# A long scan as a tree of block matmuls, a convolution as a 64-wide-tile transform, and a computed instruction order

## The chip, the cores and the metric

The kernel runs on one core of one Trainium2 chip. The metric is the device time of one execution in microseconds (us). The kernel before takes 355.92 us (median of 2 runs, 354.24 to 357.6). Profiled executions are quoted by their span, from the first to the last instruction, which is some 2 us shorter than the time. TensorE's clock is not constant: the profile gives the granted share of full speed, and each run is marked fast or slow from it and from the other runs of the same kernel.

## The reference

Two independent sequence mixers read inputs of 2048 steps x 640 channels, and their results stand side by side in the output.

```python
# part A: diagonal complex state space model, 640 states, 2048 steps
Lam_bar = exp(dt * (Lambda_re + 1j * Lambda_im))
B_bar   = ((Lam_bar - 1) / Lam)[:, None] * Bmat
Bu      = einsum("bld,pd->blp", x, B_bar)
h       = Lam_bar * h + Bu[:, t, :]            # for every t, in order
y_A     = 2 * einsum("blp,dp->bld", hseq, Cmat).real + x * Dskip

# part B: four shift taps, a gate, a causal convolution over all 2048 steps
k_shift = sum_t k[t - j] * shift_k[:, j]       # j = 0..3
kv      = k_shift * v
y_B     = q * (causal_conv(kv, ssm_k) + kv * ssm_D)
```

## The kernel before

Part A runs as 5 state tiles x 4 chunks of 512 steps. In each block TensorE multiplies by B, ScalarE copies the result out of PSUM (where the matmuls put their sums), and VectorE turns the complex decay into a real one (rotate by cosines and sines, scan 512 steps, rotate back). Then TensorE projects with C.

```python
def block(self, j, c):                         # 20 of these (cut)
    for k in range(NT):
        nc.tensor.matmul(pz[:, 0, :], lhsT=self.BTre[:, k, j * 128:(j + 1) * 128], rhs=xT[:, k, :], ...)
    ...                                        # the same for BTim
    nc.scalar.copy(out=z[:], in_=pz[:])
    nc.vector.tensor_tensor(out=t1[:], in0=cosT, in1=zre, op=ALU.mult)
    ...                                        # six such 512-wide operations
    nc.vector.tensor_tensor_scan(out=ure[:], data0=rb, data1=wre[:], initial=ini_re, ...)
    nc.vector.tensor_tensor_scan(out=uim[:], data0=rb, data1=wim[:], initial=ini_im, ...)
    ...                                        # six more to rotate back: hre, him
```

Part B is a 4096-point transform of the padded sequence in two stages, and VectorE does the taps and the products.

```python
for j in (2, 1, 0):                            # taps
    nc.vector.scalar_tensor_tensor(out=kvT[:], in0=kT[:, PAD - j:PAD - j + L], scalar=sk[:, j:j + 1], in1=kvT[:], ...)
...
nc.tensor.matmul(pa[:, i, :], lhsT=st[:, d8, a_lo * 128:(a_lo + 1) * 128], rhs=self.C.R[:, a_lo, :], ...)  # 128x512
nc.scalar.copy(out=As[...], in_=pa[...])
```

The order of instructions is that of the program, which mixes blocks of part A into part B after a fixed pattern.

Of the kernel before, what the change touches and what calls it, by code (L numbers as in the profile page):

```python
# [9 lines left out]
ALU = mybir.AluOpType  # L10
ACT = mybir.ActivationFunctionType
# [3 lines left out]
PI = float(np.pi)  # L15
TWO_PI = float(2 * np.pi)
MAGIC = 12582912.0
SC = float(2 * np.pi / 2 ** 32 * (1 - 2 ** -22))
NFFT = 4096

L = 2048
D = 640
NT = 5
CW = 512
NCH = L // CW
PAD = 16
PGROUPS = [[0, 16, 1, 2], [3, 4, 5, 6], [7, 8, 9, 10], [11, 12, 13, 14], [15]]
PLANE_POS = {k1: i for i, k1 in enumerate([0, 16] + list(range(1, 16)))}


class BConstants:

    def __init__(self, nc, cpool, tpool, hpi_col):
        self.nc, self.cpool, self.tp, self.hpi = nc, cpool, tpool, hpi_col
        g, v = nc.gpsimd, nc.vector
        self.pidx_i = tpool.tile([128, 1], i32, name="pidx_i")
        g.iota(self.pidx_i[:], pattern=[[0, 1]], base=0, channel_multiplier=1)
        self.plo_i = tpool.tile([128, 1], i32, name="plo_i")
        v.tensor_single_scalar(out=self.plo_i[:], in_=self.pidx_i[:], scalar=7, op=ALU.bitwise_and)
        self.phi_i = tpool.tile([128, 1], i32, name="phi_i")  # L40
        v.tensor_single_scalar(out=self.phi_i[:], in_=self.pidx_i[:], scalar=3, op=ALU.arith_shift_right)
        self.c20 = tpool.tile([128, 1], i32, name="c20")
        g.iota(self.c20[:], pattern=[[0, 1]], base=2 ** 20, channel_multiplier=0)
        self.c27 = tpool.tile([128, 1], i32, name="c27")
        g.iota(self.c27[:], pattern=[[0, 1]], base=2 ** 27, channel_multiplier=0)

    def _cos(self, out_ap, ph, shape, tag):
        aph = self.tp.tile(shape, f32, name=f"{tag}_aph")
        self.nc.scalar.activation(out=aph[:], in_=ph, func=ACT.Abs, scale=SC)
        self.nc.scalar.activation(out=out_ap, in_=aph[:], func=ACT.Sin, bias=self.hpi[:, 0:1], scale=-1.0)  # L50

    def _kq_iota(self, shape, pat_slot, pat_part, tag):
        g, tp = self.nc.gpsimd, self.tp
        kcol = tp.tile(shape, i32, name=f"{tag}_kcol")
        g.iota(kcol[:], pattern=pat_slot, base=0, channel_multiplier=0)
        q8 = tp.tile(shape, i32, name=f"{tag}_q8")
        g.iota(q8[:], pattern=pat_part, base=0, channel_multiplier=0)
        return kcol, q8

    def build_R(self):  # L60
        nc, tp, g = self.nc, self.tp, self.nc.gpsimd
        sh = [128, 16, 2]
        kcol, q8 = self._kq_iota(sh, [[1, 16], [0, 2]], [[0, 16], [8, 2]], "r")
        g.iota(kcol[:, 0:1, 1:2], pattern=[[0, 1], [0, 1]], base=16, channel_multiplier=0)
        g.iota(q8[:, 0:1, 1:2], pattern=[[0, 1], [0, 1]], base=0, channel_multiplier=0)
        gcol = tp.tile([128, 16], i32, name="r_gcol")
        g.iota(gcol[:], pattern=[[1, 16]], base=0, channel_multiplier=0)
        mask = tp.tile([128, 16], bf16, name="r_mask")
        nc.vector.tensor_tensor(out=mask[:], in0=gcol[:], in1=self.phi_i[:, 0:1].to_broadcast([128, 16]), op=ALU.is_equal)

        def bc(t):
            return t[:, 0:1].to_broadcast([128, 32]).rearrange("p (s t) -> p s t", s=16)

        a2 = tp.tile([128, 1], i32, name="r_a2")
        g.tensor_tensor(out=a2[:], in0=self.plo_i[:], in1=self.plo_i[:], op=ALU.add)
        m = tp.tile(sh, i32, name="r_m")
        g.tensor_tensor(out=m[:], in0=kcol[:], in1=bc(a2), op=ALU.mult)
        g.tensor_tensor(out=m[:], in0=m[:], in1=q8[:], op=ALU.add)
        self.R = self.cpool.tile([128, 2, 512], bf16, name="R")
        for a_lo in range(2):  # L80
            if a_lo == 1:
                g.tensor_tensor(out=m[:], in0=m[:], in1=kcol[:], op=ALU.add)
            ph = tp.tile(sh, i32, name="r_ph")
            g.tensor_tensor(out=ph[:], in0=m[:], in1=bc(self.c27), op=ALU.mult)
            cv = tp.tile([128, 32], bf16, name="r_cv")
            self._cos(cv[:].rearrange("p (s t) -> p s t", s=16), ph[:], sh, "r")
            g.tensor_tensor(out=self.R[:, a_lo, :].rearrange("p (g k) -> p g k", k=32),
                            in0=cv[:].rearrange("p (o k) -> p o k", o=1).to_broadcast([128, 16, 32]),
                            in1=mask[:].rearrange("p (g o) -> p g o", o=1).to_broadcast([128, 16, 32]), op=ALU.mult)

    def build_G(self):
        nc, tp, g = self.nc, self.tp, self.nc.gpsimd
        bsh = tp.tile([128, 1], i32, name="g_bsh")
        nc.vector.tensor_single_scalar(out=bsh[:], in_=self.pidx_i[:], scalar=20, op=ALU.logical_shift_left)
        self.Gre = self.cpool.tile([128, 17, 128], bf16, name="Gre")
        self.Gim = self.cpool.tile([128, 17, 128], bf16, name="Gim")
        self.nGim = self.cpool.tile([128, 15, 128], bf16, name="nGim")
        for (p0, p1) in ((0, 3), (3, 6), (6, 9), (9, 12), (12, 15), (15, 17)):
            n = p1 - p0
            sh = [128, n, 128]  # L100
            v = tp.tile([128, 3, 128], i32, name="t_v")
            g.iota(v[:, 0:n, :], pattern=[[1, n], [32, 128]], base=p0, channel_multiplier=0)
            ph = tp.tile([128, 3, 128], i32, name="t_ph")
            g.tensor_tensor(out=ph[:, 0:n, :], in0=v[:, 0:n, :], in1=bsh[:, 0:1].to_broadcast([128, n * 128]).rearrange(
                "p (a b) -> p a b", a=n), op=ALU.mult)
            nc.scalar.activation(out=self.Gim[:, p0:p1, :], in_=ph[:, 0:n, :], func=ACT.Sin, scale=-SC)
            q0 = max(p0, 1)
            q1 = min(p1, 16)
            nc.scalar.activation(out=self.nGim[:, q0 - 1:q1 - 1, :], in_=ph[:, q0 - p0:q1 - p0, :], func=ACT.Sin, scale=SC)
            aph = tp.tile([128, 3, 128], f32, name="t_aph")  # L110
            nc.scalar.activation(out=aph[:, 0:n, :], in_=ph[:, 0:n, :], func=ACT.Abs, scale=SC)
            nc.scalar.activation(out=self.Gre[:, p0:p1, :], in_=aph[:, 0:n, :], func=ACT.Sin, bias=self.hpi[:, 0:1], scale=-1.0)

    def build_H(self):
        nc = self.nc
        self.Hre = self.cpool.tile([128, 17, 128], bf16, name="Hre")
        self.nHim = self.cpool.tile([128, 17, 128], bf16, name="nHim")
        self.Him = self.cpool.tile([128, 15, 128], bf16, name="Him")
        nc.sync.dma_start_transpose(out=self.Hre[:], in_=self.Gre[:])
        nc.sync.dma_start_transpose(out=self.nHim[:], in_=self.Gim[:])  # L120
        nc.sync.dma_start_transpose(out=self.Him[:], in_=self.nGim[:])

    def build_Mq(self):
        nc, tp, g, v = self.nc, self.tp, self.nc.gpsimd, self.nc.vector
        kap = tp.tile([128, 4], i32, name="m_kap")
        g.iota(kap[:], pattern=[[8, 4]], base=0, channel_multiplier=0)
        g.tensor_tensor(out=kap[:], in0=kap[:], in1=self.plo_i[:, 0:1].to_broadcast([128, 4]), op=ALU.add)
        slot = tp.tile([128, 4], i32, name="m_slot")
        v.tensor_single_scalar(out=slot[:], in_=kap[:], scalar=1, op=ALU.arith_shift_right)
        part = tp.tile([128, 4], i32, name="m_part")  # L130
        v.tensor_single_scalar(out=part[:], in_=kap[:], scalar=1, op=ALU.bitwise_and)
        eq1 = tp.tile([128, 4], i32, name="m_eq1")
        v.tensor_single_scalar(out=eq1[:], in_=kap[:], scalar=1, op=ALU.is_equal)
        kcol = tp.tile([128, 4], i32, name="m_kcol")
        v.tensor_single_scalar(out=kcol[:], in_=eq1[:], scalar=4, op=ALU.logical_shift_left)
        v.tensor_tensor(out=kcol[:], in0=kcol[:], in1=slot[:], op=ALU.add)
        q8 = tp.tile([128, 4], i32, name="m_q8")
        v.tensor_tensor(out=q8[:], in0=part[:], in1=eq1[:], op=ALU.subtract)
# [13 lines left out]
        def bq(t):  # L152
            return t[:].rearrange("p (q o) -> p q o", o=1).to_broadcast(sh3)
# [15 lines left out]
class PartA:  # L169
# [155 lines left out]
    def block(self, c, j, base0=None):  # L325
# [67 lines left out]
        if j == NT - 1:  # L393
            self.project(c)
# [308 lines left out]
```

## Time and profile before

| kernel before, profiled span 354.2 us | TensorE | VectorE | ScalarE | GpSimd |
|---|---|---|---|---|
| busy, us | 235.3 | 282.7 | 173.1 | 85.3 |

The next lines are from the page of the kernel before: busy time of each engine with its share of the span, then three rows of the strip in which each digit is the busy share, in tenths, of one fortieth of the span (8.9 us), or the granted TensorE clock in tenths, then the shares of the chain of waits.

```profile
span 354.2 us, 5098 instructions
...
PE 235.3 (66%) x1896; PEld 150.7 (43%) x1896; DVE 282.7 (80%) x619; ACT 173.1 (49%) x231; POOL 85.3 (24%) x99
...
PE   0058179303799874757898198588499997675591
DVE  3809999984999999998970799999974896989502
PEclk9998859856699999699999789589699999699698
...
issue 36%; DVE 24%; POOL 12%; PE 9%; SPq 8%; DMA 6%; ACT 3%; ACTq 1%; POOLq 0%; DVEq 0%
```

VectorE (DVE) is the limit: row after row of nines, and the engine with the largest busy share. TensorE (PE) is busy for 66% of the span; its longest wait in total is for VectorE, as the next lines show.

Two groups of the same page show what TensorE waits for, and one more thing that is easy to overlook. A group line gives busy time, mean ns of one instruction, and the idle time before it with the engine that ended it.

```profile
L406 PE MATMUL psA<-Csre,hre 128*128 128x320 bf16 x160 | 49.2, 330 | 40.8 <-DVE hre L388 21.0
...
L161 POOL TENSOR_TENSOR m_cv<-m_cv,m_coef 128x64 f32<-128x64 f32 x1 | 25.2, 25237 | 4.1 <-ACT m_cv L50 4.1
```

The projection waits 21.0 us for the rotated state on VectorE. And one GpSimd (POOL) multiply of 128x64 elements took 25.2 us beside a full VectorE.

### The profile page before, as it was taken

To read this page: it belongs to the slowest core of one execution; us is meant where nothing else is said; L and a number is where in the kernel's file an instruction comes from. 1 tells how busy PE (TensorE), PEld (TensorE's weight loads), DVE (VectorE), ACT (ScalarE), POOL (GpSimd) and SP (SyncE) were. 2 spreads that over 40 slices of the span, in tenths; PEclk is the share of its full clock that TensorE was granted. 3 is DMA by queue.
4 is the path that set the end of the run, shared out by engine and by line. 5 is a ranking of instruction groups with operands and counts; after the bars stand their busy time and mean duration, and the time that the engine had idled before them with its cause. 6 is when DMAs were issued, how large, how long until landed. Compare 5 with 4: busy or idle time off the path is not lost.

```text
span 354.2 us, 5098 instructions
## 1 busy us (share of the span) xinstructions
PE 235.3 (66%) x1896; PEld 150.7 (43%) x1896; DVE 282.7 (80%) x619; ACT 173.1 (49%) x231; POOL 85.3 (24%) x99
## 2 busy tenths in 40 slices
PE   0058179303799874757898198588499997675591
PEld 0013055301564542544655065265286554464371
DVE  3809999984999999998970799999974896989502
ACT  3548748303357484246564216478254795245020
POOL 2943639993120000020210001001041000020021
PEclk9998859856699999699999789589699999699698
DMA  5999997101035544283757704020664012232312
GB/s 95 197 209 213 205 213 150 44 0 61 19 102 141 112 105 108 71 161 64 179 137 153 170 1 121 20 71 30 148 166 149 1 31 54 66 102 61 76 57 78
DMA packets 89802, 36.68 MB, mean 104 GB/s; under 512 B 76465, under 2 KB 86706, under 8 KB 89778
## 3 DMA queue, kind: packets, MB, share of 16 engines
q1 hardware_dynamic: 65330, 18.01, 25.6%
q0 software_dynamic: 3808, 13.11, 12.5%
q10 hardware_dynamic: 20640, 5.24, 6.5%
q8 instruction: 15, 0.25, 0.3%
q14 instruction: 9, 0.07, 0.1%
HBM read 9.19 MB, written 6.55 MB: 44 GB/s over the span
## 4 chain that ended last, share of the span: by engine, by line
issue 36%; DVE 24%; POOL 12%; PE 9%; SPq 8%; DMA 6%; ACT 3%; ACTq 1%; POOLq 0%; DVEq 0%
POOL m_cv L161 7%; DVE kvT L495 4%; DVE uim L377 2%; PE psB L452 2%; DVE ure L376 2%; SPq L483 2%; DMA Zt<-Zs 2%; DMA out_dram<-yo 2%; PE psB L593 2%; SPq L500 1%; PE psA L406 1%; DMA vT<-in_B_v_dram 1%; PE psA L407 1%; SPq L209 1%; ACTq L583 1%
## 5 line engine op out<-in xcount | busy, mean ns | idle before, releaser
L406 PE MATMUL psA<-Csre,hre 128*128 128x320 bf16 x160 | 49.2, 330 | 40.8 <-DVE hre L388 21.0
L352 PE MATMUL psA<-xT,BTre 128*128 128x512 bf16 x100 | 31.1, 417 | 32.5 <-DMA xT<-in_A_x_dram 20.9
L407 PE MATMUL psA<-Csimn,him 128*128 128x320 bf16 x160 | 49.1, 327 | 1.3 <-DVE him L391 1.2
L337 POOL DMA_DIRECT2D tbase<-trig_tab x15 | 10.8, 721 | 120.4 <-DVE sct L348 75.5
L535 ACT CAST Xs<-psB 128x1024 bf16<-128x1024 f32 (+1 forms) x25 | 21.9, 886 | 36.1 <-PE psB L475 18.5
L358 ACT CAST z<-psA 128x1024 bf16<-128x1024 f32 x20 | 20.1, 1014 | 26.4 <-PE psA L355 15.5
L407 PEld LDWEIGHTS <-him 128*128 128x128 bf16 x160 | 16.7, 105 | 30.2 <-issue 18.7
L406 PEld LDWEIGHTS <-hre 128*128 128x128 bf16 x160 | 16.4, 105 | 30.2 <-DVE hre L388 24.4
L352 PEld LDWEIGHTS <-BTre 128*128 128x128 bf16 x100 | 10.1, 104 | 43.6 <-issue 25.6
L593 PE MATMUL psB<-Mq,Zt 128*128 128x256 bf16 x160 | 24.3, 323 | 6.6 <-DMA Zt<-Zs 6.6
L452 PE MATMUL psB<-R,h_st 128*128 128x512 bf16 x80 | 24.6, 449 | 5.9 <-ACT As_h L454 2.1
L514 ACT CAST Hf<-psB 128x1024 bf16<-128x1024 f32 (+1 forms) x25 | 21.0, 891 | 15.2 <-PE psB L475 10.6
L355 PE MATMUL psA<-xT,BTim 128*128 128x512 bf16 x100 | 27.7, 391 | 0.0
L161 POOL TENSOR_TENSOR m_cv<-m_cv,m_coef 128x64 f32<-128x64 f32 x1 | 25.2, 25237 | 4.1 <-ACT m_cv L50 4.1
L418 ACT CAST yo<-psA 128x640 bf16<-128x640 f32 x16 | 11.0, 694 | 28.6 <-PE psA L415 22.9
L454 ACT CAST As_h<-psB 128x1024 bf16<-128x1024 f32 x20 | 19.9, 1012 | 9.4 <-PE psB L452 9.4
L595 DVE TENSOR_TENSOR ob<-psB,qin 128x1024 bf16<-128x1024 f32 x10 | 12.1, 1217 | 15.0 <-PE psB L593 15.0
L593 PEld LDWEIGHTS <-Zt 128*128 128x128 bf16 x160 | 18.5, 117 | 12.8 <-DMA Zt<-Zs 7.5
L420 POOL DMA_DIRECT2D out_dram<-yo x16 | 8.9, 559 | 55.0 <-ACT yo L418 54.9
L344 ACT ACTIVATE tbA<-tbase,rot_s 128x512 bf16<-128x512 bf16 x15 | 10.9, 725 | 22.7 <-DVE sct L347 19.0
L598 POOL DMA_DIRECT2D out_dram<-ob x5 | 5.9, 1178 | 63.6 <-DVE ob L595 63.6
L581 ACT CAST Zs<-psB 128x1024 bf16<-128x1024 f32 x20 | 19.6, 1011 | 1.4 <-PE psB L580 1.4
(629 smaller groups left out, 780.9 us busy)
## 6 DMA issues: line engine op xcount, KB each, us to landing
tbase<-trig_tab POOLq DMA_DIRECT2D x15, 256.0 KB, 3.3
qin<-in_B_q_dram POOLq DMA_DIRECT2D x5, 512.0 KB, 6.3
h_st<-in_B_ssm_k_dram SPq DMA_DIRECT2D x40, 64.0 KB, 2.1
kv_st<-kvT SPq DMA_DIRECT2D x40, 64.0 KB, 2.4
out_dram<-yo POOLq DMA_DIRECT2D x16, 160.0 KB, 2.1
out_dram<-ob POOLq DMA_DIRECT2D x5, 512.0 KB, 4.6
trig_tab<-tb_base POOLq DMA_DIRECT2D x5, 256.0 KB, 5.0
kT<-in_B_k_dram SPq DMA_TRANSPOSE x5, 6.7
```

Of the source, the lines that this page charges most:

```text
L161: g.tensor_tensor(out=cv[:], in0=cv[:], in1=bq(coef), op=ALU.mult)
L352: nc.tensor.matmul(pz[:, 0, :], lhsT=self.BTre[:, k, j * 128:(j + 1) * 128], rhs=xT[:, k, :], start=(k == 0), stop=(k == NT - 1))
L355: nc.tensor.matmul(pz[:, 1, :], lhsT=self.BTim[:, k, j * 128:(j + 1) * 128], rhs=xT[:, k, :], start=(k == 0), stop=(k == NT - 1))
L358: nc.scalar.copy(out=z[:], in_=pz[:])
L406: nc.tensor.matmul(py[:, b, 0:320], lhsT=Hs[j][0][:, ts], rhs=self.Csre[:, j, c0:c0 + 320], start=(j == 0), stop=False)
L407: nc.tensor.matmul(py[:, b, 0:320], lhsT=Hs[j][1][:, ts], rhs=self.Csimn[:, j, c0:c0 + 320], start=False, stop=False)
L452: nc.tensor.matmul(pa[:, i, :], lhsT=st[:, d8, a_lo * 128:(a_lo + 1) * 128], rhs=self.C.R[:, a_lo, :], start=(a_lo == 0), stop=(a_lo == 1))
L454: nc.scalar.copy(out=As[:, :, 32 * pr:32 * pr + 32].rearrange("p k (i g) -> p k i g", i=2), in_=pa[:].rearrange("p i (g k) -> p k i g", k=32))
L514: nc.scalar.copy(out=Hf[:, :, pos * 128:(pos + n) * 128], in_=pt[:, :, 0:n * 128])
L535: nc.scalar.copy(out=Xs[:, :, 0:W], in_=pt[:, :, 0:W])
L581: nc.scalar.copy(out=Zs[:, qd, :, :].rearrange("p s (c k) -> p s c k", k=8), in_=pzf.rearrange("p (k s c) -> p s c k", k=8, s=8))
L593: nc.tensor.matmul(pyf[:, s4 * 256:(s4 + 1) * 256], lhsT=Zt[:, qd, st_, :], rhs=C.Mq[:, qd, :], start=(qd == 0), stop=(qd == 3))
```

## The change

The intent is to take VectorE's load away and to keep TensorE fed.

- Part A: each state of 2x64 rows is one tile of 128 rows. Steps are combined in a tree with block matrices that are powers of the decay (1, 2, 4, 8, 12 steps) and sit in PSUM accumulation. Only one step in 16 goes through a real scan on VectorE (the "coarse" scan), then the states in between are filled in by more matmuls and PSUM adds.
- Part B: the convolution is taken modulo x^2048+i, so the transform has 2048 complex points and no padding. Its matmuls are 64 wide and are placed in quarters or halves of the array.
- Order: the program first builds a graph of operations with assumed durations, list-schedules it, picks the engine of each PSUM copy (ScalarE or VectorE) and every buffer, and then emits the instructions in that order.

```diff
-        nc.vector.tensor_tensor_scan(out=ure[:], data0=rb, data1=wre[:], initial=ini_re, ...)
-        ...                                           # 20 blocks of 512-wide rotations and scans
+        for b in range(2):                            # up-sweep of tile j, half hf
+            for k in range(5):
+                nc.tensor.matmul(P[:, b, :], lhsT=self.BbT[:, j, k, :], rhs=self.xT[:, k, hf, 2*b:2*b+2, :]..., ...)
+        self.evac(f"e1_{u}", 512, ...)                # copy on ScalarE or VectorE
+        nc.tensor.matmul(self.P(pt)[:, 1, :]..., lhsT=M[1][:, j, :], rhs=self.hb[:, j, 0:3:2, ms], start=False, ...)
+        self.evac(f"e2_{u}", 256, ...)                # ... then M[2], M[4], M[8], M[12] and two more copies
+        v.tensor_tensor_scan(out=vv[:, i, :], data0=self.rn[:, 5, j:j+1]..., data1=t1[:, i, :], ...)   # 128 long
@@ convolution, first stage: 32 matmuls of 64x64
-        nc.tensor.matmul(pa[:, i, :], lhsT=st[:, d8, a_lo*128:(a_lo+1)*128], rhs=self.C.R[:, a_lo, :], ...)
+        nc.tensor.matmul(P[64*ri:64*ri+64, r, 128*b4:128*b4+128], lhsT=d[64*r:64*r+64, 4*qd+b4, a0, :],
+                         rhs=self.R[64*r:64*r+64, a0, ri, :], start=(a0 == 0), stop=(a0 == 1))
@@ the order (cut)
+    SEM = 0.12
+    def schedule(self, slots, ordered_tags, free_tags):
+        ...            # of all ready operations the one that can start first; ties by the wished time ("due")
+                    if b.tag in next_alloc and self.alloc_order[b.tag][next_alloc[b.tag]] is not b:
+                        ok = False                    # SBUF buffers are handed out in program order
+def act_c(n): return 0.19 + 0.000833 * n              # assumed durations, us
+def dve_p(n): return 0.19 + 0.00104 * n
+        op(f"x{hf}{s_}", {"SP": 0.6}, f, w=[...], dma=1.7)
+    DUE = dict(a0=15.0, a1=4.4, c0=62.0, d0=66.0, ..., bo=(0.0, 4.0, 24.0, 28.0, 36.0, 48.0))
+        order = self.g.schedule({"8": 5, "4": 8, "P": 4, "Y": 2}, ("8", "4"), ("P", "Y"))   # P: two-bank PSUM tiles
```

## The prediction

> **What bounds the kernel now.** The busy table gives the vector engine (DVE) 283 of 354 us (80%), TensorE 235 (66%), ScalarE 173 (49%). The stretch table shows DVE full (40.0 of 40 us in 100–140, 39.2 in 220–260) but not everywhere: 25.6 of 40 in 180–220 and 28.6 in 260–300, and at the end (330–354) only 5.1 of 24 while TensorE drains the last projection. TensorE's longest waits are for DVE (hre 21.0 us) and the x load (20.9). So: DVE-bound, with a ragged start, some order stalls and a tail.
>
> By line, the 20 rotated-scan blocks cost DVE about 172 us: twelve 512-wide multiplies/adds (99 us summed, 0.34 us pitch), two scans of 1.27 us (50.6 in all), and two table rotations (22.1). The convolution's spectral products cost 57 us, its shift taps 45, output multiplies 12.
>
> **What the change does to each engine** (estimates from these durations).
>
> DVE: the scan blocks shrink to two 640-wide coarse rotations with 128-long scans (about 13 us) and ten down-sweeps of four PSUM adds (about 27). Spectral products become fewer and 1024–2048 wide (about 36). Taps become scale plus add instead of 2.35 us scalar-tensor-tensors (about 40, partly on ScalarE). Output 12, set-up 20. Sum near 150.
>
> PSUM evictions: 100 of 1024 columns for the convolution at 1.01 us, 14 for constants, 20 up-sweep units of four small evictions (about 1.6 us each), 16 outputs at 0.69: near 160 us, now shared by ScalarE and DVE. With ScalarE set-up, both together hold about 320 us, so 160 each if balanced. That replaces 283 on one engine.
>
> TensorE: projection (113k columns) and first products (102k) stay; the tree adds about 45k; the convolution falls from about 246k to 123k columns if 64-wide tiles run side by side. Sum near 395k columns. This trace streams 128 columns in 55 ns at full clock, so 165 us, or about 187 at this run's mean clock 0.877. Without side-by-side tiles I estimate 80–90 us more.
>
> The Trainium skill, "TensorEngine Tiling (Array Packing)", Key Properties, says that changing tiling mode drains TensorE; no trace here shows it yet. The list order interleaves full and tiled groups (around 290 groups), so I allow 15–30 us.
>
> **Critical path.** The bottleneck moves from DVE to TensorE (about 190–210 us with drains), with DVE and ScalarE close behind at 160–175. Start-up of 10–15 us before dense matmuls, fixed engine order against real latencies, four PSUM slots, and a tail of a few us come on top. I expect 225 us.
>
> **Prediction: 225 us, 80% range 195 to 268.** Faster by over 2%: 0.95; within 2%: 0.02; slower: 0.03.
>
> **What would show each step right or wrong.** DVE busy falls to 150–180 us and ScalarE rises to 150–175. TensorE's busy share is highest, above 80%, with little idle in mid-span. A 32-matmul tiled group starts and ends within about 0.5–0.7 us (side by side) or 1.8 us (not). Full-clock share stays near 0.9.
>
> **What would make it wrong.** Tiles that serialize: 260–290 us. POOL work starved by DVE: here one 128x64 POOL multiply took 25.2 us beside a full DVE; the Trainium skill, "GPSIMD Engine Reference", Specifications, names a shared SBUF interface, and this agrees. Set matrices or a small POOL add could stall a whole chain. The load queue: here SP took 2.4–6.5 us to issue one transposing load, far more than the order assumes, so the first 30 us may slip. If all runs to plan, 195.

## The result, and the profile after

The changed kernel takes 292.22 us (median of 2 runs, 291.43 to 293.0); the ratio to the kernel before is 0.8229, 95% interval 0.8098 to 0.836. Ratios are the mean time of one kernel's fast runs over that of the other's in the same rounds, so they are not quite the ratio of the medians quoted. The direction was right, and the time is outside the predicted range of 195 to 268.

| profiled | predicted | after |
|---|---|---|
| TensorE busy, us | 190 to 210 | 208.6 |
| VectorE busy, us | 150 to 180 | 182.1 |
| ScalarE busy, us | 150 to 175 | 151.4 |
| TensorE share of the span | over 80% | 72% |
| granted clock | near 0.9 | 0.918 |
| span, us | about 223 (from 225) | 289.7 |

The same lines of the page of the changed kernel:

```profile
span 289.7 us, 8552 instructions
...
PE 208.6 (72%) x3814; PEld 143.4 (50%) x3814; DVE 182.1 (63%) x327; ACT 151.4 (52%) x198; POOL 27.9 (10%) x51
...
PE   0003488889669997439899961487899979999694
DVE  6567969224983859894753599968626697057030
PEclk9999979999968999758999977559999979999999
...
PE 47%; DVE 28%; ACT 12%; SPq 4%; issue 4%; DMA 3%; DVEq 0%; ACTq 0%
```

Every engine's load is close to what was predicted. What is not there is an engine that is full. TensorE is idle for 289.7 - 208.6 = 81.1 us. The strip shows where: three empty slices at the start, and two holes in the middle (slices 17 to 18 and 25 to 26, each of 7.2 us), where the clock row falls to 5 to 7 as well.

The table of stretches gives the same by stage (columns: length, busy us and number of instructions of each engine, granted clock, DMA share, GB/s).

```profile
0.00:20.00 20.00, 0.00 (x0) 0.00 (x0) 13.10 (x63) 7.92 (x13) 10.01 (x27) 1.00 0.76 108
20.00:40.00 20.00, 8.55 (x61) 6.64 (x62) 14.34 (x29) 11.14 (x16) 7.19 (x7) 0.93 1.12 223
...
120.00:140.00 20.00, 12.97 (x235) 8.28 (x234) 13.86 (x22) 11.25 (x13) 1.54 (x3) 0.68 0.64 128
...
180.00:200.00 20.00, 12.77 (x237) 8.68 (x237) 17.23 (x25) 6.13 (x7) 1.29 (x2) 0.65 0.67 158
```

In the first 40 us TensorE is busy for 8.55 us, so 31.5 us of the idle time lie there and 49.6 us later. In the two holes of the middle no engine is full: TensorE 13 of 20, VectorE 14 and 17, ScalarE 11 and 6. Work waits for work.

The table of waits of TensorE from 40 us on names the longest (total, times, longest):

```profile
PE ps L752 <- DVE Qb L738: 5.5, 1, 5.5
PE ps L714 <- DVE cw L729: 4.4, 1, 4.4
PE ps L752 <- DVE hb L769: 4.3, 1, 4.3
```

L714 to L752 are the coarse scan and the first matmul of the down-sweep: a serial chain of VectorE steps with TensorE at both ends, and in these stretches the order had nothing else ready for TensorE. The Trainium skill, page "TensorE: Matmul & The Clock Gate", section "HAM oscillation", says that idle gaps of more than about 3.4 us throttle TensorE's clock. This trace agrees in part. The wait of 4.4 us ends at 178.4 and that of 5.5 us at 184.6, and from 184.6 to 194.1 the granted clock is 0.50, so these waits were paid a second time in slower matmuls. But before the wait of 4.3 us (123.7 to 127.9) the clock was halved already, as the next lines show, and in the 5 us before 119 no wait was longer than 0.93 us; TensorE was busy for only 2.35 of the 4 us there. So many short waits went before this loss of clock, and the long one only lies inside it.

```profile
115.00:119.00 4.00, 2.35 (x10) 0.88 (x9) 3.93 (x6) 3.06 (x5) 0.00 (x0) 1.00 0.00 0
119.00:123.60 4.60, 2.03 (x20) 1.28 (x20) 3.86 (x7) 3.75 (x5) 0.00 (x0) 0.51 0.01 4
...
133.00:140.00 7.00, 6.44 (x164) 3.93 (x162) 3.68 (x7) 4.35 (x5) 0.37 (x2) 1.00 1.37 229
```

At the start, these lines of the timeline (start, duration, instruction, idle time before and what ended it) show the way to TensorE's first matmul:

```profile
15.33 1.03 DVE L547 CAST sk<-sk_b 128x20 f32<-128x20 bf16 x1 [2.56 <-DMA sk_b<-in_B_shift_k_dram]
...
19.64 1.15 ACT L532 ACTIVATE s<-s,mpi 128x1024 f32<-128x1024 int32 x1 [3.84 <-DVE s L528]
...
22.92 0.24 ACT L330 ACTIVATE aph<-ph 128x60 f32<-128x60 int32 x1
...
23.56 0.22 DVE L340 TENSOR_TENSOR rc<-rn,cs 128x60 f32<-128x60 f32 x1 [3.55 <-ACT cs L332]
...
26.44 2.72 PE L630 MATMUL ps<-s,s 128*128 128x128 bf16 x24 [26.44 <-DVE s L422]
```

VectorE, which takes its queue in order, stops for a small load that only part B needs; behind it waits a step of a large table; ScalarE stops for that step, and behind it stand the three small sines and cosines (L330 to L332) that the state matrices need. Read like this, the start is held by order and not by load; the experiments below test that, and it is not confirmed.

What had been doubtful came out well. Tiles do run side by side: two groups of 32 small matmuls take 1.09 us, as this line shows, so 0.55 for each, inside the predicted 0.5 to 0.7. The projection, which waited 21.0 us for VectorE before (group L406), now waits 2.0 (second line; the old GpSimd multiply has no counterpart).

```profile
62.57 1.09 PE L918 MATMUL ps<-R,s 64*64 64x128 bf16 x64
```

```profile
L823 PE MATMUL ps<-BC,hb 128*128 128x320 bf16 x240 | 36.8, 302 | 2.0 <-DVE s L236 2.0
```

The theory formed from this reading, A: no engine and no shared resource holds the time; the order of the instructions and of the buffers does, in the middle through chains with nothing beside them and at the start through small steps behind unready ones. Its rival, B: the engines disturb one another (semaphores, the port that VectorE and GpSimd share, drains, transfers), and the idle time stays whatever the order.

### The profile page after: what moved, and what is told of

It reads as the page before. It is cut to its first block, busy times and chain, and to the rows that moved or that the text cites. A ratio compares the mean times of both kernels' runs of the same rounds, so it can differ in the third digit from the quotient of the medians.

```text
span 289.7 us, 8552 instructions
## 1 busy us (share of the span) xinstructions
PE 208.6 (72%) x3814; PEld 143.4 (50%) x3814; DVE 182.1 (63%) x327; ACT 151.4 (52%) x198; POOL 27.9 (10%) x51
## 4 chain that ended last, share of the span: by engine, by line
PE 47%; DVE 28%; ACT 12%; SPq 4%; issue 4%; DMA 3%; DVEq 0%; ACTq 0%
PE ps L667 13%; PE ps L823 11%; ACT s L234 7%; DVE s L977 6%; PE ps L918 6%; PE ps L954 5%; PE ps L1048 4%; SPq L602 3%; PE ps L1010 3%; DVE M L422 3%; DVE s L893 3%; DVE R L757 3%; DVE s L236 3%; DMA s<-s 2%; DVE hb L769 2%
## 5 line engine op out<-in xcount | busy, mean ns | idle before, releaser
L234 ACT CAST s<-ps 128x1024 bf16<-128x1024 f32 x87 | 83.9, 1021 | 38.9 <-PE ps L918 16.9
L667 PE MATMUL ps<-xT,BC 128*128 128x512 bf16 x200 | 49.0, 384 | 1.0 <-ACT s L234 0.8
L823 PE MATMUL ps<-BC,hb 128*128 128x320 bf16 x240 | 36.8, 302 | 2.0 <-DVE s L236 2.0
L977 DVE TENSOR_TENSOR s<-s,s 128x1024 bf16<-128x1024 bf16 (+1 forms) x30 | 25.1, 866 | 7.8 <-ACT s L234 7.5
L823 PEld LDWEIGHTS <-hb 128*128 128x128 bf16 x240 | 22.0, 98 | 10.4 <-issue 2.0
L918 PE MATMUL ps<-R,s 64*64 64x128 bf16 x1280 | 24.7, 235 | 3.0 <-ACT s L234 2.2
L918 PEld LDWEIGHTS <-s 64*64 64x64 bf16 x1280 | 22.2, 119 | 8.2 <-issue 7.5
L630 PE MATMUL ps<-s,s 128*128 128x128 bf16 x50 | 6.2, 309 | 26.4 <-DVE s L422 26.4
L954 PE MATMUL ps<-s,Wre 128*64 128x128 bf16 x320 | 22.0, 227 | 4.1 <-ACT s L234 2.7
L885 ACT ACTIVATE s<-s,sk 128x1024 bf16<-128x1024 bf16 x16 | 18.1, 1150 | 7.7 <-DVE s L893 4.3
L954 PE MATMUL ps<-s,Wim 128*64 128x128 bf16 x320 | 21.7, 224 | 0.0
L893 DVE TENSOR_TENSOR s<-s,s 128x1024 bf16<-128x1024 bf16 x30 | 19.4, 686 | 0.2
```

The lines of the kernel that those rows point to most:

```text
L234: self.nc.scalar.copy(out=out, in_=in_)
L630: self.nc.tensor.matmul(P[:, q // 4, 128 * (q % 4):128 * (q % 4) + 128], lhsT=bv(j // 5)[:, j % 5, 128 * k:128 * k + 128], rhs=self.mgv()[ ...
L667: nc.tensor.matmul(P[:, b, :], lhsT=self.BbT[:, j, k, :], rhs=self.xT[:, k, hf, 2 * b:2 * b + 2, :] .rearrange("p s m -> p (s m)"), start= ...
L823: nc.tensor.matmul(P[:, part, 0:320], lhsT=hap(j), rhs=self.CT[:, j, c0:c0 + 320], start=(j == 0), stop=False)
L885: nc.scalar.activation(out=out, in_=k(j), func=ACT.Copy, scale=self.sk[:, G, j:j + 1])
L893: op(f"ca{j}{G}{h}", {"DVE": dve_tt(1024)}, lambda e, c=c, tt=tt: v.tensor_tensor(out=c(), in0=c(), in1=tt(), op=ALU.add), r=[f"tm{G}{h}"] ...
```

## The experiments

Each kernel was timed beside the kernel before on its own chip, so compare ratios across groups.

### slots3: one PSUM tile fewer

```diff
-        self.psl = [self.ps.tile([128, 2, 512], f32, name=f"ps_{i}") for i in range(4)]
+        self.psl = [self.ps.tile([128, 2, 512], f32, name=f"ps_{i}") for i in range(3)]
-        order = self.g.schedule({..., "P": 4, ...})
+        order = self.g.schedule({..., "P": 3, ...})
```

> Three double-bank PSUM buffers instead of four, everything else as in the changed kernel (the list order is drawn up again for three). Theory A, the order itself is the limit: the kernel's own list schedule grows from 277.3 to 291.1 us, and a replay of both orders with durations measured in the trace of the changed kernel says 294 against 309 us. So about 302 to 309 us, 10 to 17 us over the changed kernel's 292. Theory B, engine work is the limit and PSUM buffers are deep enough: within 3 us of 292.

Measured: 306.59 us (306.3 to 309.92), ratio 0.8563 [0.8487, 0.8639], TensorE busy 212.3 of 304.5. The work is the same and the time is 14 us longer; by the ratios (0.8563 against 0.8229), which allow for the other chip, about 12 us. That is theory A's range: waits for buffers, and the new order drawn up for them, show in the time. The Trainium skill, page "Perfetto Trace Analysis", section "Matmul Optimizations", asks that all eight PSUM banks be used; here six banks instead of eight cost these 12 us.

### bank_tiles: three two-bank tiles and two one-bank tiles

The copy after the first five matmuls of an up-sweep unit waited for the next five too, which go to the other bank of the same tile. Tiles of one bank take this false wait away, in the same eight banks.

```diff
+        self.pss = [self.ps.tile([128, 512], f32, name=f"pt_{i}") for i in range(2)]
-        pt = self.g.buf("P", "pu" + u)
+        pts = [self.g.buf("S", f"pu{b}" + u) for b in range(2)]
```

> PSUM split into three double-bank tiles and two single-bank tiles; the up-sweep and down-sweep of the scan use single banks, so that the first copy of a unit no longer waits for the second group of five matmuls of that unit, which write another bank of the same tile. The list schedule's own end hardly moves (277.3 to 275.3 us). Theory: the wait for the second group is false and costs TensorE 0.6 to 0.8 us in a unit where nothing else is ready; replay with measured durations: 284 us, 8 to 10 us under the changed kernel. Rival: the wait is hidden by other work, so no change beyond 3 us (289 to 292).

Measured: 291.78 us (289.72 to 294.04), ratio 0.815 [0.8073, 0.8227]. That is the rival's number; against the ratio of the changed kernel (0.8229) the gain is about 1%, and the intervals overlap. No effect is shown.

### conv_only and scan_only: each part alone (wrong results on purpose)

```diff
@@ conv_only                                 @@ scan_only
-        self.a_loads(); self.a_bbar(); ...   -        self.b_load(0); self.b_conv(0); ...
```

> Only the convolution half runs (wrong result on purpose: the scan half of the output is not written). Engine work of this half is about 120 us each on ScalarE and DVE and 63 us on TensorE. Theory A, a group of 128 channels is a serial chain and the buffer rule of the list lets the groups overlap little: 215 to 225 us (own schedule 219.8, replay 221). Theory B, engine work sets the time: 140 to 155 us.

> Only the scan half runs (wrong result on purpose: the convolution half of the output is not written). TensorE work is about 120 us, DVE 83, ScalarE 57. Theory A, latency of the chains of one unit after another and of the coarse scan shows: 185 to 200 us (own schedule 173.7, replay with measured durations 201). Theory B, engine work sets the time: 140 to 155 us.

Measured, one run each (state unknown): 233.49 and 195.49 us. Scan_only is in theory A's range; conv_only is 8.5 us above it, with TensorE at a mean granted clock of 0.759. Here are the busy lines of conv_only and then scan_only.

```profile
span 231.7 us, 6401 instructions
...
PE 90.7 (39%) x2880; PEld 86.2 (37%) x2880; DVE 128.2 (55%) x229; ACT 111.9 (48%) x122; POOL 23.4 (10%) x42
```

```profile
span 193.7 us, 2336 instructions
...
PE 136.2 (70%) x934; PEld 78.7 (41%) x934; DVE 85.9 (44%) x187; ACT 51.9 (27%) x97; POOL 15.1 (8%) x29
```

Alone, neither part fills any engine. That fits two chains, with the kernel's speed set by how well they are laid over each other: 233 + 195 = 429 us one after the other, 292 together.

### control, replan_costs, replan, replan_start: the same instructions in another order

These four ran on one chip. The work is the same in all; since the schedule also chooses engines, some operations move (in replan VectorE has 320 instructions instead of 327, GpSimd 67 instead of 51). In replan_costs the scheduler assumes the durations that its trace showed, lets transfers run all at once instead of one after another, and counts with a unit's first copy waiting for both groups of matmuls; in replan its wished times were searched again with them; replan_start mends the start as well.

```diff
@@ replan_costs
+    def calibrate(self):                 # called before schedule()
+        ...  x loads {"SP": 2.45}; zt {"SP": 4.9}; i1 PE 1.1; state matrices DVE 0.85, POOL 1.9; V {"SP": 7.7}; ...
-    SEM = 0.12
+    SEM = 0.2
-                b0 = max(fin, dma_free)                            # transfers one after another
+                b0 = fin                                           # all at once
@@ replan: the above, and
-    DUE = dict(a0=15.0, a1=4.4, c0=62.0, ..., bo=(0.0, 4.0, 24.0, 28.0, 36.0, 48.0))
+    DUE = dict(a0=7.54, a1=6.78, c0=53.54, ..., bo=(-0.3, 4.9, 25.5, 27.5, 34.2, 48.1))
@@ replan_start: the above with its own wished times, and parameter loads and B first, k taps ahead
```

> The changed kernel itself, on the chip of the three runs beside it. Both theories: ratio to the kernel before 0.81 to 0.835, so about 290 to 297 us, and a profile like the one shown (TensorE about 208 us busy).

> The same instructions and buffers; only the durations that the kernel's scheduler assumes are replaced by those its trace showed, with the same wished times. Theory A (the order and the order of the buffers, chosen with wrong durations, hold the time, not any engine): the scheduler now plans 275 against 290 to 294 for the old order timed with the same durations, so 272 to 283 us. Rival B (the engines disturb one another; whatever the order, about 80 us of TensorE idle time stay): within 2% of the control. Busy sums of all engines within 3% of the control in both.

> As the run before, and the wished times of the groups of operations were searched again with the measured durations: no instruction is added or taken away, only the order and with it the buffer use differ. The scheduler plans 247. Theory A: 247 to 262 us, TensorE's idle time down from about 81 to 40 to 55 us with its busy time unchanged near 208. Rival B: within 2% of the control. In between (265 to 280): both hold in part.

> Replanned like the run before, and besides the start is mended: the small parameter loads ahead of the transposing loads, the loads of B given their buffers first, the first set of state matrices kept in a tile of its own, and the next group's loads and taps placed ahead of this group's second transform stage. The scheduler plans 245. Theory A: 244 to 260 us, TensorE's first matmul at 15 to 21 us instead of 26.4. Rival B: within 2% of the control.

| run | time, us | ratio [95%] | TensorE busy, idle, us |
|---|---|---|---|
| control | 292.12 | 0.8265 [0.8204, 0.8326] | 208.1, 81.2 |
| replan_costs | 288.15 | 0.8132 [0.8066, 0.8198] | (profiled run slow) |
| replan | 271.75 | 0.7664 [0.76, 0.7729] | 205.3, 64.3 |
| replan_start | 283.77 | 0.8027 [0.7968, 0.8086] | 204.1, 79.6 |

Right durations with the old wished times gave 1.6%, which is rival B's number. New wished times with the same instructions gave 7%, between the two theories' numbers. So the order (with the choice of engines that goes with it) is a cause, but it was not all of it in this form. The idle time after 40 us fell from 49.6 to 27.9 us (229.6 us less 201.75 busy); in the first 40 us it rose from 31.5 to 36.5.

replan_start missed its expectation by 24 us, and its trace shows why: VectorE stood 8.89 us behind the load of k and TensorE's first matmul came at 43.6 us instead of 26.4. An operation that was put early in a queue because its load "should be there by then" stops everything behind it when the load is late.

The replan run also shows what GpSimd costs VectorE. Both built state matrices (L422) at the same time; VectorE first, GpSimd second:

```profile
22.11 0.82 DVE L422 TENSOR_TENSOR s<-E,sg 128x640 bf16<-128x640 bf16 x1
...
29.60 7.55 DVE L422 TENSOR_TENSOR s<-E,sg 128x640 bf16<-128x640 bf16 x1
```

```profile
30.36 6.10 POOL L422 TENSOR_TENSOR M<-E,ss 128x640 bf16<-128x640 bf16 x5
```

The same VectorE instruction takes 0.82 us alone and 7.55 us beside five GpSimd instructions in a row. The Trainium skill, page "SBUF — State Buffer", section "SBUF: two separate sides", says that the two engines share a port pair under an exclusive lock, so that the loser blocks instead of sharing. The trace agrees that one of the two is blocked, and shows that it can stay so through several instructions of the other; here it was even the one that started first by the profile (29.60 against 30.36). The copy that TensorE needed next stood behind it on VectorE, and TensorE idled 10.3 us, of which this can explain some 6.7.

### plain_x and replan2_plain_x: plain loads instead of transposing ones (wrong results on purpose)

```diff
-                    src = self.x2[1024 * hf + r:1024 * hf + 1024:4, :].rearrange("t (k d) -> t k d", d=128)
-                    nc.sync.dma_start_transpose(out=self.xT[:, :, hf, s_, :], in_=src)
+                    src = self.x2[1024 * hf + 256 * s_:1024 * hf + 256 * s_ + 256, :].rearrange("(p u) d -> p (u d)", u=2)
+                    nc.sync.dma_start(out=self.xT[:, :, hf, s_, :], in_=src.rearrange("p (k e) -> p k e", e=256))
```

> The changed kernel in its own order with one edit, wrong on purpose: the eight transposing loads of x, 2.4 us each on the queue of SyncE, become plain loads of as many bytes. Theory A (the start is held by what waits behind those loads on that queue and in the transfer engines): TensorE's first matmul moves from 26.4 to 15 to 20 us and the time falls by 6 to 12 us, to 280 to 286. Rival B (the start is held by the parameter arithmetic on VectorE and ScalarE itself, 18 us of small dependent steps): first matmul at 24 to 27 us, time within 1% of the changed kernel.

> The kernel of the run replan2, order unchanged, wrong on purpose: the eight transposing loads of x become plain loads of as many bytes. In replan2 seven of them held SyncE's queue from 2.9 to 18.9 us, and k, v and B came after. If the transfers of the start hold what is left (theory A): k lands about 6 us earlier, TensorE's idle time in the first 45 us falls from about 29 to 20 to 25, time 260 to 266 us. Rival B (the parameter arithmetic and its order hold the start): 267 to 273 us, within 1.5% of replan2.

Measured: plain_x 291.81 us (ratio 0.82 [0.8148, 0.8252]), replan2_plain_x 269.18 us (0.7542 [0.7476, 0.7609], against 0.7591 [0.7519, 0.7663] for replan2). The loads did get shorter on the queue of SyncE, as the first lines below show for the changed kernel and the second for plain_x (with TensorE's first matmul below it); the time did not.

```profile
2.91 9.69 SPq L602 DMA_TRANSPOSE xT<-in_A_x_dram  x4
```

```profile
2.88 5.96 SPq L602 DMA_DIRECT2D xT<-in_A_x_dram  x4
...
26.73 2.72 PE L630 MATMUL ps<-s,s 128*128 128x128 bf16 x24 [26.73 <-DVE s L422]
```

TensorE's first matmul comes at 26.7 instead of 26.4. The small load behind the loads of x was issued 3.1 us earlier (9.56 against 12.65), but took 5.0 us to land instead of 2.7, and VectorE's cast behind it 2.19 us instead of 1.03, so VectorE got past it no sooner. In replan2_plain_x the load of k left the queue 5 us earlier (18.2 against 23.2), and TensorE's idle time in the first 45 us stayed at 31.2 us (31.3 in replan2), where theory A expected 20 to 25. The length of the transposing loads, which the prediction feared, does not hold the start.

### replan2, replan2_start and replan3: what the traces of these runs taught, put into the scheduler

```diff
@@ replan2 (wished times searched again)
+            if n[:4] == "set_":   o.alts = {"DVE": 0.85}           # state matrices on VectorE alone
+            elif b == "kv":       a["SP"], o.dma = 0.4, 2.5        # longer transfers for k, v and the round trip
-        small("diagD", ..., 0.8)
+        small("diagD", ..., 0.8, due=60)
@@ replan2_start: the above, and loads of B before k and v, shift taps' load first on ScalarE
@@ replan3: replan2, and
-                b0 = fin                                           # all transfers at once
+                b0 = max(fin, dma_free) if o.dma > 0.2 else fin    # large transfers one after another
-        op("ld_sk", {"SP": 0.6, "POOL": 1.0}, ...)
+        op("ld_sk", {"ACT": 0.7}, ..., due=-90)                    # small loads first, on ScalarE's queue
+                    out=(self.cw[h][:] if key == "G" else ...)     # first state matrices in a tile of their own
```

> Like the run replan (same instructions), with what that run's trace showed put into the scheduler: the state matrices all on VectorE (beside GpSimd they took 1.5 us each instead of 0.83, in the very stretch in which TensorE stood 10.3 us), the scaled identity (4.9 us) wished for later, longer transfers assumed for k, v and the round trip through DRAM. Planned 248. Theory A (wrong durations in the plan are what is left to mend by order alone): 258 to 266 us, TensorE idle in its first 45 us down by 6 to 10. Rival B (what is left is set by transfers and the engines' sharing, not by order): within 1.5% of 271.8.

> Like replan2, and besides: the load of the shift taps first on ScalarE's queue, the loads of B given their buffers before k and v, the first state matrix set in a tile of its own. Not the reordered parameter loads that spoiled the run replan_start. Planned 246. Theory A: 255 to 264 us. If the early loads of B again delay k as in replan_start (k landed 18.4 us after issue there): 270 or more.

> Planned once more, with a scheduler that lets large transfers follow one another instead of all at once (with that model the order of replan2 comes to 264, against 267.5 in its profile), with the three small loads that blocked VectorE issued first and from ScalarE, and the first set of state matrices in a tile of its own. Planned 257. If order still holds the start (theory A): 258 to 265 us. If the transfers hold it whatever the order (rival B): 266 to 272 us. If an early load is late again and blocks an engine's queue, as in replan_start and replan2_start: over 274.

Measured: replan2 269.28 us, ratio 0.7591 [0.7519, 0.7663], TensorE idle in its first 40 us 30.0 instead of 36.5. The time is the rival's (within 1.5% of replan), although the start did improve as theory A said: the 6.5 us gained there do not show in the time (34.5 us idle after 40 us, against 27.9). How much was lost later is not certain: 24 of the 3814 matmuls are missing from the trace of replan2, some 5 us of work that counts as idle here. replan2_start 279.55 us, ratio 0.7843 [0.7778, 0.7908]: it failed like replan_start, VectorE standing 18.1 us at a load of 1.2 KB, issued by GpSimd, that landed 22.2 us after its issue beside the large ones.

(Of the three small loads of replan3's text, those of the shift taps and of part B's D went to ScalarE; that of part A's D stayed on GpSimd's queue.) replan3 is the fastest of the three: 261.81 us (260.23 to 262.8), ratio 0.7329 [0.7271, 0.7386]. Its page, its stretches 0 to 40 and 40 to the end, and its longest waits from 40 us on:

```profile
span 258.5 us, 8534 instructions
...
PE 196.8 (76%) x3814; PEld 135.8 (53%) x3814; DVE 179.4 (69%) x325; ACT 153.2 (59%) x203; POOL 27.2 (11%) x54
...
PE   0000519999869989666989977779999789999973
...
PEclk9999999999999999999999997999999999999998
```

```profile
0.00:40.00 40.00, 6.00 (x169) 5.78 (x171) 29.77 (x95) 21.36 (x28) 12.86 (x31) 1.00 1.06 152
40.00:400.00 360.00, 190.79 (x3651) 129.97 (x3646) 149.64 (x231) 131.87 (x177) 14.32 (x23) 0.99 0.35 77
```

```profile
PE ps L918 <- ACT s L235: 3.5, 6, 1.1
PE ps L1010 <- ACT s L235: 2.5, 5, 0.7
PE ps L1048 <- DMA s<-s: 2.1, 2, 1.7
```

The waits of 4.3 to 5.5 us after 40 us are gone, the longest of these three is 1.7 us, and the clock row has lost its holes: 0.990 granted instead of 0.918. The 0.990 is somewhat too high: in the first 40 us, where the row says 9, the first 128 small matmuls took 3.96 us (next line), against 1.09 for 64 at full clock in the changed kernel. The trace's first clock record lies at 41.6 us, and what comes before it counts as full speed. The other three executions of replan3 have 0.963 to 0.974.

```profile
25.59 3.96 PE L918 MATMUL ps<-R,s 64*64 64x128 bf16 x128 [25.59 <-DVE R L492]
```

After 40 us TensorE is idle for 27.7 us instead of 49.6. And the same matmuls are busy for 196.8 us instead of 208.6, because they run at a higher clock (busy time times clock: 194.8 and 191.5). The number is the one theory A expected, but not for the reason given there: the start is not shorter (34.0 us of idle time in the first 40). A time that falls into the expected range proves the mechanism only if the stretch in question moved too.

### replan4b, replan4b_no_sets, replan5, replan5_k_first: what holds the start

These change replan3's order by hand.

```diff
@@ replan4b: after schedule()
+        mv = ["ld_ldt0", "ld_ldt1", "ld_lre0", "ld_lre1", "ld_lim0", "ld_lim1"]   # parameters before other small loads
+        rest[i:i] = [by[n] for n in mv]
+        rest.insert(... "set_12_1" ... + 1, by["diagD"])                          # scaled identity after the matrices
@@ replan4b_no_sets (wrong on purpose): each state matrix writes a fifth of its tile, the rest is cleared at the start
@@ replan5: replan4b, and
+        rest.insert(... "g" ... + 1, by["sk"])                                    # cast of the taps later too
@@ replan5_k_first: replan5, and
+        new = iter([by["k0"], by["v0"]] + xs)                                     # k and v before the loads of x
```

> The kernel of the run replan3 with its order changed in two places by hand and nothing else: the three parameter loads of ScalarE's queue come before the loads of the shift taps and of D, and the scaled identity (needed only by the projection, after 100 us) comes after the state matrices. In replan3 VectorE stood 6.2 us, from 8.95 to 15.11, at the head of its queue for the small load behind that identity, with all parameter arithmetic behind it. Theory A (VectorE's in-order queue holds the start): TensorE's first matmul at 18 to 21 us instead of 25.6, its idle time in the first 40 us down from 34 to 26 to 30, time 254 to 259 us. Rival B (the transfers of x, k, v and B hold the start): first matmul earlier, but idle time in the first 40 us within 2 us and the time within 1% of replan3.

> replan4b, wrong on purpose: each of the twelve operations that build the state matrices (0.83 us each on VectorE, ten of them before 40 us) writes one fifth of its tile, and the rest is cleared at the very start, where VectorE waits for parameters anyway. The same order, loads and matmuls. Theory A (VectorE's own set-up work stands in series with TensorE at the start): another 4 to 8 us off the time of replan4b. Rival B (transfers): within 1% of replan4b.

> replan4b with one more operation moved: the cast of the shift taps on VectorE, which in replan4b stood 7.3 us (to 16.2) at the head of the queue for a load of 5 KB issued at 3.2 us that landed 13.0 us later, goes behind the parameter arithmetic. Theory C (the start is held by small loads that land late beside the large ones, through the in-order queue of VectorE): the chain starts at 11 to 12 us, when the last parameter lands, TensorE's first matmul at 20 to 22 instead of 25.8, its idle time in the first 40 us down by 3 to 5 us, time 253 to 257. Rival B (k, v, x and B themselves hold it): first matmul earlier, time within 1% of 259.

> replan5 with k and v of the first group ahead of the eight loads of x on SyncE's queue (x is first read after 41 us in this order). Theory B (large loads in the wrong order hold the start): k lands near 9 to 12 instead of 22 us, the taps follow as soon as theirs have landed, and the time falls another 2 to 5 us below replan5. Theory C alone: within 1% of replan5.

replan4b: 259.14 us, ratio 0.731 [0.7242, 0.7379] (the record's own verdict on it and on replan4b_no_sets is "unclear"); idle time in the first 40 us 34.2, first matmul at 25.8. The time is rival B's, within 1% of replan3, but the test did not do what it was for: the wait moved to the next small load. VectorE's line, and the line of that load in the list of transfers (KB, us from issue to landing):

```profile
16.19 0.18 DVE L547 CAST sk<-sk_b 128x20 f32<-128x20 bf16 x1 [7.33 <-DMA sk_b<-in_B_shift_k_dram]
```

```profile
sk_b<-in_B_shift_k_dram ACTq DMA_DIRECT2D x1, 5.0 KB, 13.0
```

A load of 5 KB took 13.0 us beside the large ones; in the changed kernel, issued later, the same load took 2.7.

replan5: 259.9 us, ratio 0.7291 [0.7231, 0.735]. Now VectorE does not stop for it: TensorE's first matmul comes at 22.93 and the idle time in the first 40 us is 31.6 us (40 less 8.36 busy), 2.6 less than in replan4b. The time did not fall with it; theory C expected 253 to 257 us. replan5_k_first: the three fast runs give 0.7371 [0.7304, 0.7439], not faster; a fourth run of it took 413.39 us and is left out as slow. It is the one that was profiled: k left SyncE's queue at 11.1 us instead of 19.6 (replan5), and still TensorE's first matmul came at 23.7. Its trace holds no clock record, so the clock of 1.0 in its result says nothing: its matmuls of 512 columns start 444 ns apart, 216 in the changed kernel. TensorE ran at about half speed throughout; why is open. replan4b_no_sets: only two fast runs, 258.74 and 255.91, ratio 0.726 [0.714, 0.738]; inconclusive, where theory A expected another 4 to 8 us. So the start stays open. These runs show that it is neither the transposing form of the x loads, nor the order of k and v against x, nor VectorE's queue alone. What most of them share is a VectorE that is full while TensorE starts, 19.6 to 19.8 of the 20 us from 20 to 40 in replan, replan3, replan4b and replan5 (in replan2 17.9, and in the changed kernel 14.3). That this is the limit there is a reading and was not proved.

The fastest versions, replan3, replan4b and replan5, cannot be told apart by their intervals, and their intervals lie below that of the changed kernel: about 0.73 of the kernel before.

## Why the prediction was right or wrong

- **That the kernel gets faster by over 2%, and that VectorE stops being the limit:** right. VectorE's busy time fell from 282.7 to 182.1 us, 2 us over the predicted 150 to 180.
- **The loads of the other engines:** right as totals. ScalarE 151.4 us (150 to 175), TensorE 208.6 (190 to 210), the latter in part by luck: its terms were off, as the point on drains shows.
- **Tiles side by side:** right, 0.55 us for a group of 32.
- **15 to 30 us of drains between tiling modes:** there, but smaller. The Trainium skill, page "TensorEngine Tiling (Array Packing)", section "Key Properties", says that a change of mode drains TensorE. The trace shows a delay at each change, in the starts (ends are modelled and overlap). Below, pairs of 128x64 tiles start every 0.055 us, but the first full matmul comes 0.16 us after the last pair:

```profile
106.87 0.22 PE L954 MATMUL ps<-s,Wre 128*64 128x128 bf16 x2
106.92 0.22 PE L954 MATMUL ps<-s,Wim 128*64 128x128 bf16 x2
107.08 0.34 PE L689 MATMUL ps<-Qb,M 128*128 128x64 bf16 x3
```

Over the 77 changes of the changed kernel's trace at full clock and without a wait, the next start comes about 0.1 us (median) later than the columns before it need; between one group of full matmuls and the next it is typically 0.002 to 0.003. The trace has 109 changes, not 290, so this is an estimate of about 10 us in all. No run isolates it. The columns explain less than the sum says too: at 55 ns for 128, 395k columns are 170 us, or 185 at the granted clock of 0.918, and 208.6 were busy. What else makes the difference is not shown.
- **GpSimd starved by VectorE:** the sharing is real, but the victim was the other one: VectorE waited for GpSimd (7.55 us for an instruction of 0.82).
- **The load queue:** VectorE did stop for small loads that landed late beside large ones (2.56 us in the changed kernel, 7.33 in replan4b), but neither removing such a stop nor shortening the transposing loads (291.8 us with plain ones) shortened the time.
- **The step that failed:** "Start-up of 10–15 us before dense matmuls, fixed engine order against real latencies, four PSUM slots, and a tail of a few us come on top. I expect 225 us." With TensorE at about 200, this allowed about 25 us of TensorE idle time in all. It was 81.1: 31.5 in the first 40 us, and 49.6 later. The mechanism was named, its size was not worked out. The prediction added up each engine's work and took the largest sum, as if the others could always be hidden behind it. But three engines with loads of 209, 182 and 151 us that feed one another left TensorE waiting.
- **What the runs showed in its place:** of the 49.6 us after the start, a new order of the same work recovers 22 (27.9 in replan), and in replan3 the higher clock that goes with fewer gaps gives another 12 (208.6 to 196.8 busy). One PSUM tile fewer costs about 12. In all, order brought 292 us down to 262; of the 67 us above the predicted 225, some 37 stay. Of the 31.5 us at the start no correct kernel tried recovered more than 1.5 (replan2, 30.0), and what holds it stays open.
- **TensorE's share above 80%:** wrong for the same reason, 72%; even replan3 has 76%.

## What to carry to other kernels

When a change takes the load off the one full engine, do not predict the next largest sum: ask for each stretch what TensorE has ready while a serial chain runs elsewhere, and count the start as a chain of its own. A computed order is only as good as the durations and the latencies it assumes, and it is worth computing again with those of its own trace: here the same work went from 292 to about 260 us (new durations alone gave 1.6%, a new search for the wished times the larger part). In an engine's in-order queue nothing that waits for a load may stand ahead of work that does not need it.

## What the Trainium skill lacked or had wrong

- Page "DMA: Bandwidth & Descriptors" (section "Latency and other measured facts") gives first-byte latencies of about 0.6 to 1 us and up to 2 us from a loaded memory, but not how late a small load lands beside large ones: 13.0 us for 5 KB in replan4b, 2.7 us for the same load in the changed kernel.
- No page gives the time for which a transposing load of this size holds the issuing queue (the DMA page has cycle counts for other cases only): about 2.4 us each here (9.69 for four), against 1.5 for plain loads of the same bytes (5.96 for four). Page "Advanced Engine Details and Errata", section "X-Bar Transpose (TRN2)", calls both equally fast; from issue to landing they are here too (6.9 and 7.0 us), so the difference is in the issuing queue alone.
- Page "SBUF — State Buffer" says that the loser of the shared port blocks for the winner's instruction, and that whichever starts first wins. The run replan shows one blocked through five instructions of the other, 7.55 us for an instruction of 0.82, though by the profile it had started first.
- Page "TensorEngine Tiling (Array Packing)" warns of a drain at each change of tiling mode and gives no size; here the next start comes about 0.1 us later at such a change.
- Page "TensorE: Matmul & The Clock Gate" is right about gaps for the waits of 4.4 and 5.5 us, but in the changed kernel the clock was also halved at 119 us with no wait above 0.93 us in the 5 us before. The size in a real kernel may be added: TensorE was busy for 208.6 us at a clock of 0.918 over the span, and for 196.8 us at a recorded 0.990.
